# Linear attention in front of two feed-forward stages: scores in 64x64 pieces without the masked quarter, every second tile's decayed k on VectorE, v loaded without padding

## The chip, the cores and the metric

The kernel runs on one core of a Trainium2 chip. The metric is the device time of one execution in microseconds (us), the median of several runs. The engines are called as the profile calls them: PE (TensorE matmul), PEld (its weight loads), DVE (VectorE), ACT (ScalarE), POOL (GpSimd) and SP (SyncE, which here only issues transfers).

## What is computed

Three stages follow one another. The first is a linear attention with decay for 4 sequences of 768 tokens and 8 heads of 48, written in the reference as a loop over tokens:

```python
for t in range(S):
    kt, vt, rt = (k[:, :, t], v[:, :, t], r[:, :, t])
    cur = np.einsum('bhd,bhe->bhde', u[None] * kt, vt)
    y[:, :, t] = np.einsum('bhd,bhde->bhe', rt, state + cur)
    state = w[None, :, :, None] * state + np.einsum('bhd,bhe->bhde', kt, vt)
```

Its output (3072 tokens of 384) goes to a mixture of 8 experts, where each token takes the expert of its largest logit, and from there to a gated feed-forward layer `(silu(x @ w_gate) * (x @ w_val)) @ w_out`.

## The kernel before

**The first stage** works on 24 tiles of 128 tokens, 6 for each sequence. Inside a tile the loop over tokens is a matrix product. r is scaled by powers of the decay (`rdT`), k by inverse powers (`kdT`), both with heads on the partitions, two heads to a pair (rows 0 to 63 and 64 to 127, 48 of each 64 used). The scores of a pair are `kdT` times `rdT`, 128 keys by 128 queries. Only keys before the query count, so half of that square is masked away: `copy_predicated` on DVE puts the scores where the mask is 1 into `dsb`, which holds a diagonal elsewhere (the bonus term with u, from `ck` and its sum `cb`). `psy` is v times `dsb`, plus the state of the earlier tiles times `rdT`. The state itself takes `kdc` (k by token, scaled to the tile's end) times v in `pskv`. `psx` turns the result round and computes the gate logits.

**Who does what in a tile.** POOL makes `ck` in two products, `kdT`, and `kdc` for five tiles in six. DVE makes `rdT`, sums `ck` into `cb`, does two `copy_predicated`, a small sum of logits, and four updates of the state; after each sequence it also does the routing of its tokens in small steps (`advance()`), which stand between the others. ACT makes the eight diagonals of `dsb` from `cb`, and copies `psy` and `psx` out of PSUM. PE does `pss` (scores), `pskv`, `psy` (two lines), `psx`.

**Order.** On PE, DVE, ACT and POOL the instructions of this stage are taken in the order in which the program writes them. The loop runs over `i`; `scaled_r(i + 1)` and `bonus(i + 1)` stand ahead of `scores(i)`, then come `state(i - 1)`, `scaled_k(i + 2)`, `outputs(i - 1)` and `rows_out(i - 2)`. So POOL works two tiles ahead of the scores and DVE one tile ahead. `kdT`, `kdc` and `dsb` have three buffers, `ck` two, the loaded tiles three; `pss` has two PSUM banks that every tile uses again, except tile 1, which has two of its own. SP issues the loads of tile `i + 3` when the instructions that read tile `i` are done.

The second stage starts with a gather of the routed tokens while the last tiles are finished; from there on PE works through the experts and the feed-forward layer.

Of the kernel before, what the change touches and what calls it, by code (L numbers as in the profile page):

```python
# [20 lines left out]
P = 128  # L21
# [17 lines left out]
def moe_kernel(ctx, tc, cst, small, tok, tr, u, w1, w2, m_gate, m_val, m_out, out):  # L39
# [281 lines left out]
    with ExitStack() as actx:  # L321
# [23 lines left out]
            t = bank[:, places[name]]  # L345
            return t if len(dims) == 1 else t.rearrange("p (a b) -> p a b", b=dims[1])

        RK, V, T = 2 * H * D, H * 64, NP * P
        NIO, NV = 3, 4
        io = [carve(RK + 2 * T) for _ in range(NIO)]  # L350
        io_v = [carve(V) for _ in range(NV)]

        def load(i):
            if i < NTILE:
# [3 lines left out]

        def load_v(i):
            if i < NTILE:  # L360
                nc.sync.dma_start(out=io_v[i % NV], in_=tok[i, :, RK:])

        def heads(ap, d=D):
            return ap.rearrange("p (h d) -> p h d", d=d)
# [5 lines left out]
        load(0)  # L370
        nc.sync.dma_start(out=u_tok, in_=u.rearrange("(o h) d -> o h d", o=1).to_broadcast([P, H, D]))
        nc.sync.dma_start(out=cs, in_=cst)
        for i in range(1, NIO):
            load(i)
            load_v(i - 1)
# [13 lines left out]
        def powers():  # L389
            nc.vector.memset(ones, 1.0)  # L390
            nc.vector.memset(pw[:, :, 0:1], 1.0)
            for t in kdc_b:
                nc.gpsimd.memset(t[:, :, D:], 0.0)

            for i in range(WARM):
                wu = ps_m.tile([P, 512], F32, name="wu", tag="m")
# [12 lines left out]
            for q in range(NP):  # L409
                nc.vector.reciprocal(wkT[:, q, :], pw[:, q, 1:])  # L410
                nc.scalar.mul(we[:, q, :], wkT[:, q, :], pw[:, q, P : P + 1])
            pst = ps_m.tile([P, NP, P], F32, name="pst", tag="m")
            for q in range(NP):
                nc.tensor.transpose(pst[:, q, :], we[:, q, :], ident)
            nc.scalar.copy(wk_tok, pst.rearrange("p q (j d) -> p (q j) d", j=2)[:, :, 0:D])
# [23 lines left out]
                )  # L439
            nc.gpsimd.tensor_copy(unit[:, :, D:], wg[:, :, 0:G])  # L440

        S = {}

        def inputs(i):
            t = io[i % NIO]
            r_t, k_t = heads(t[:, 0 : RK // 2]), heads(t[:, RK // 2 : RK])
            rT, kT = pairs(t[:, RK : RK + T]), pairs(t[:, RK + T :])
            rdT = apool.tile([P, NP, P], F32, name="rdT", bufs=3)
            kdT = apool.tile([P, NP, P], F32, name="kdT", bufs=3)
            ck = apool.tile([P, H, D], F32, name="ck")  # L450
            kdc = kdc_b[i % 3]
            S[i] = r_t, k_t, rT, kT, rdT, kdT, ck, kdc

        def scaled_k(i):

# [15 lines left out]
                nc.gpsimd.tensor_tensor(out=ck, in0=ck, in1=r_t, op=ALU.mult)  # L471
            if i:
                nc.gpsimd.tensor_tensor(out=kdT, in0=kT, in1=wkT, op=ALU.mult)  # L473
            if (i + 1) % NCH:
                nc.gpsimd.tensor_tensor(out=kdc[:, :, 0:D], in0=k_t, in1=wk_tok, op=ALU.mult)  # L475

        def scaled_r(i):
            if i >= NTILE:
                return
            r_t, k_t, rT, kT, rdT, kdT, ck, kdc = S[i]  # L480
            if i >= NTILE - 2:
                nc.gpsimd.tensor_tensor(out=rdT, in0=rT, in1=wrT, op=ALU.mult)
            elif i:
                nc.vector.tensor_tensor(out=rdT, in0=rT, in1=wr_ps, op=ALU.mult)
            if i == 1:
                load_v(3)
            load(i + NIO)
            if i == 0:
                load_v(2)

        def bonus(i):
# [5 lines left out]

            dsb = apool.tile([P, H, P], F32, name="dsb", bufs=3)
            for h in [*range(0, H, 2), *range(1, H, 2)]:
                nc.scalar.mul(dsb[:, h, :], ident, cb[:, h : h + 1])  # L500
            S[i] = rdT, kdT, kdc, dsb, heads(io_v[i % NV], 64)

        def scores(i):
            rdT, kdT, kdc, dsb, v_t = S[i]

            if i == 1:
                both = ps_x.tile([P, 2, NP, P], F32, name="pss01", tag="x")
                pss = [both[:, j] for j in range(2)]
            else:
                pss = [ps_s.tile([P, NP, P], F32, name=f"pss{j}", tag="s") for j in range(2)]  # L510
            for q, j in itertools.product(range(NP), range(2)):
                p0 = 64 * j
                nc.tensor.matmul(  # L513
                    pss[j][:, q, :], lhsT=kdT[p0 : p0 + 64, q, :], rhs=rdT[p0 : p0 + 64, q, :], start=True, stop=True
                )
            for j in range(2):
                nc.vector.copy_predicated(
                    dsb.rearrange("p (q j) t -> p q j t", j=2)[:, :, j, :],
                    mask.bitcast(I32).rearrange("p (o t) -> p o t", o=1).to_broadcast([P, NP, P]),
                    pss[j],  # L520
                )
                advance()
                advance()

        def state(i):
# [6 lines left out]
            for q in range(NP):  # L532
                for j in range(2):
                    p0 = 64 * j
                    nc.tensor.matmul(
                        pskv[p0 : p0 + 64, q, :], lhsT=kdc[:, 2 * q + j, :], rhs=v_t[:, 2 * q + j, :],
                        start=True, stop=True,
                    )
            if c == 0:
# [13 lines left out]
        def outputs(i):  # L553
# [4 lines left out]
            for q in range(NP):  # L558
                for j in range(2):
                    p0 = 64 * j  # L560
                    nc.tensor.matmul(  # L561
                        psy[p0 : p0 + 64, q, :], lhsT=v_t[:, 2 * q + j, :], rhs=dsb[:, 2 * q + j, :],
                        start=(q == 0), stop=(c == 0 and q == NP - 1), skip_group_check=True,
                    )
            if c > 0:
# [213 lines left out]
    def sequential(c):  # L779
# [6 lines left out]
        v_d = tok[:, :, 2 * H * D :].rearrange("i t (q j d) -> i j t q d", j=2, d=64)  # L786
# [4 lines left out]
        with tc.For_i(0, B) as b:  # L791
            nc.vector.memset(st, 0.0)
            with tc.For_i(0, NCH) as ch:
# [7 lines left out]
                with tc.For_i(0, P) as t:  # L801
                    kv = sq.tile([P, NP, D], F32, name="sq_kv")
                    for j in range(2):
                        nc.sync.dma_start(
                            out=kv[64 * j : 64 * j + 64],
                            in_=v_d[bass.ds(i, 1), j, bass.ds(t, 1), :, 0:D]
                            .rearrange("o a q d -> (o a) q d").to_broadcast([64, NP, D]),
                        )
                    r_t, k_t = (rk[:, n, :, bass.ds(t, 1)] for n in range(2))
                    nc.vector.tensor_tensor(out=kv, in0=kv, in1=bc(k_t), op=ALU.mult)  # L810
                    cur = sq.tile([P, NP, D], F32, name="sq_cur")
                    nc.vector.tensor_tensor(out=cur, in0=kv, in1=col(up), op=ALU.mult)
                    nc.vector.tensor_tensor(out=cur, in0=cur, in1=st, op=ALU.add)
                    nc.vector.tensor_tensor(out=cur, in0=cur, in1=bc(r_t), op=ALU.mult)
                    psy = ps_m.tile([P, NP], F32, name="sq_psy", tag="m")
                    for q in range(NP):
                        for p0 in (0, 64):
                            nc.tensor.matmul(
                                psy[p0 : p0 + D, q : q + 1], lhsT=cur[p0 : p0 + 64, q, :], rhs=ones[p0 : p0 + 64, :],
                                start=True, stop=True,  # L820
                            )
                    for p0 in (0, 64):
                        pr = slice(p0, p0 + D)
                        nc.vector.tensor_copy(yT[pr, :, bass.ds(t, 1)], psy[pr].rearrange("p (q o) -> p q o", o=1))
                    nc.vector.tensor_tensor(out=st, in0=st, in1=col(wp), op=ALU.mult)
                    nc.vector.tensor_tensor(out=st, in0=st, in1=kv, op=ALU.add)
# [611 lines left out]
EARLY = 3  # L1438
# [54 lines left out]
def _layout(inputs):  # L1493
# [4 lines left out]
    b, h, s, d = r.shape  # L1498
    n = s // P

    def tokens(a, pad=0):
        a = a.transpose(0, 2, 1, 3)
        if pad:
            a = np.concatenate([a, np.zeros(a.shape[:3] + (pad,), a.dtype)], axis=3)
        return a.reshape(b * n, P, -1)

    def pair_rows(a, fill):

# [6 lines left out]
    def transposed(a):  # L1515
# [7 lines left out]
    out = {  # L1523
        "cst": _constants(),
        "small": small,
        "tok": np.concatenate([tokens(r), tokens(k), tokens(v, 64 - d)], axis=2),
        "tr": np.concatenate([transposed(r), transposed(k)], axis=2),
        "u": u,
        "w1": inputs["moe_w1"],
# [27 lines left out]
```

## Time and profile before

| | us |
|---|---|
| median of 3 runs | 800.56 (798.5 to 801.65) |
| the profiled execution | 798.91 |
| its span | 797.2 |
| PE busy | 777.5, 98% of the span |
| DVE busy | 498.1, 62% |
| ACT busy | 346.8, 44% |
| POOL busy | 220.2, 28% |

The profile comes from one execution. Its time stands 1.7 above its span, and its span is what the rows count in. The shares are means over stages that differ: POOL's 28% is nearly all in the first eighth of the span, where it hardly rests. Matmuls are pipelined, so a busy PE need not be PE at its peak, and a matmul's shown length overlaps the next one's.

### The profile page before, as it was taken

The page shows a single profiled execution, that of the slowest core. Times are in us where ns is not written, and L with a number is a line of the kernel's source. Part 1 is how long each engine was busy: PE and PEld are TensorE (multiplying, and loading weights), DVE is VectorE, ACT ScalarE, POOL GpSimd, SP SyncE. Part 2 cuts the span into 40 slices and gives each one's busy share as a digit, 9 for nine tenths or more (in the row PEclk, how much of TensorE's full clock was granted, in tenths as well). Part 3 has the DMA queues.
Part 4 walks back from the last instruction along what each step waited for, and adds up shares of the span by engine and source line. Part 5 has one row for each costly group of instructions (what it writes and reads, how often), then busy time and mean ns, then how long its engine had stood idle before and what let it go on. Part 6 is the DMA issues. An engine that isn't in the chain of part 4 may idle for free.

```text
span 797.2 us, 15589 instructions
## 1 busy us (share of the span) xinstructions
PE 777.5 (98%) x5982; PEld 713.3 (89%) x5983; DVE 498.1 (62%) x1041; ACT 346.8 (44%) x785; POOL 220.2 (28%) x213
## 2 busy tenths in 40 slices
PE   8989998999999999999999999999999999999997
PEld 4878888899999999988888888888888888899997
DVE  7889976889999899787553335334433543344543
ACT  5878873656656656654432223222212221122322
POOL 6999986545233322120002000100200020001000
PEclk9999999999999999999999999999999999999999
DMA  8999974867877784564201000000100000000000
GB/s 321 307 336 339 303 268 142 289 199 220 253 239 238 248 246 144 159 191 140 89 14 40 1 0 14 40 1 1 44 9 1 7 40 1 1 8 40 1 21 24
DMA packets 61860, 99.28 MB, mean 125 GB/s; under 512 B 5461, under 2 KB 48105, under 8 KB 61776
## 3 DMA queue, kind: packets, MB, share of 16 engines
q1 hardware_dynamic: 58320, 88.34, 34.0%
q0 software_dynamic: 3456, 9.85, 3.6%
q8 instruction: 49, 0.80, 0.4%
q14 instruction: 35, 0.29, 0.1%
HBM read 81.64 MB, written 16.53 MB: 123 GB/s over the span
## 4 chain that ended last, share of the span: by engine, by line
issue 54%; PE 29%; POOL 8%; DVE 5%; DMA 1%; ACT 1%; POOLq 0%; SPq 0%; DVEq 0%; ACTq 0%
PE ph L1209 10%; PE py L1209 9%; POOL out_dram L1381 2%; PE pss L513 1%; PE psy L561 1%; POOL kdT L473 1%; POOL kdc L475 1%; PE psy L569 1%; POOL ck L470 1%; PE pya L1209 1%; PE wu L397 1%; POOL ck L471 1%; DMA rw<-m 1%; PE pt L1176 1%; PE pha L1209 1%
## 5 line engine op out<-in xcount | busy, mean ns | idle before, releaser
L1405 PE MATMUL pg<-x,wh 128*128 128x512 f32 (+1 forms) x504 | 146.6, 359 | 0.0
L1410 DVE TENSOR_TENSOR hv<-pg,hv 128x512 f32<-128x512 f32 (+1 forms) x84 | 51.6, 615 | 141.5 <-ACT hv L1409 141.4
L1405 PE MATMUL pv<-x,wh 128*128 128x512 f32 (+1 forms) x504 | 137.7, 358 | 0.0
L1381 POOL DMA_INDIRECT out_dram<-ot,tokd x24 | 24.9, 1038 | 407.1 <-DVE ot L1380 403.4
L1409 ACT ACTIVATE hv<-pg 128x512 f32<-128x512 f32 (+1 forms) x84 | 45.0, 536 | 158.5 <-PE pg L1405 158.1
L968 ACT CAST hh<-hv 128x512 fp32r<-128x512 f32 (+1 forms) x84 | 47.0, 560 | 136.7 <-DVE hv L1411 136.7
L1405 PEld LDWEIGHTS pv<-x,wh 128*128 128x128 f32 x504 | 89.9, 188 | 13.9
L1405 PEld LDWEIGHTS pg<-x,wh 128*128 128x128 f32 x504 | 90.2, 188 | 11.3
L1372 PE MATMUL po<-wh,hl 128*128 128x384 f32 x288 | 97.1, 338 | 0.0
L1372 PE MATMUL po<-wl,hh 128*128 128x384 f32 x288 | 96.8, 336 | 0.0
L1372 PE MATMUL po<-wh,hh 128*128 128x384 f32 x288 | 96.8, 336 | 0.0
L1405 PE MATMUL pg<-x,wl 128*128 128x512 f32 (+1 forms) x252 | 90.3, 358 | 0.0
L1405 PE MATMUL pv<-x,wl 128*128 128x512 f32 (+1 forms) x252 | 90.3, 358 | 0.0
L1209 PE MATMUL ph<-x,w1h 128*128 128x416 f32 (+6 forms) x336 | 87.5, 341 | 0.0
L1209 PE MATMUL py<-h,w2h 128*128 128x416 f32 (+6 forms) x336 | 82.4, 341 | 0.0
L969 DVE TENSOR_TENSOR hl<-hv,hh 128x512 fp32r<-128x512 f32 (+1 forms) x84 | 51.7, 616 | 43.6 <-ACT hh L968 43.3
L1411 DVE TENSOR_TENSOR hv<-pv,hv 128x512 f32<-128x512 f32 (+1 forms) x84 | 51.7, 615 | 38.5 <-PE pv L1405 37.9
L500 ACT ACTIVATE dsb<-cs,cb 128x128 f32<-128x128 f32 x192 | 58.7, 390 | 16.2 <-DVE cb L496 16.0
L1209 PEld LDWEIGHTS ph<-x,w1h 128*128 128x128 f32 x336 | 61.5, 188 | 0.2
L1209 PEld LDWEIGHTS py<-h,w2h 128*128 128x128 f32 x336 | 60.7, 188 | 0.5 <-DVE h L1229 0.3
L1050 POOL TENSOR_TENSOR low<-low,exw 128x384 f32<-128x384 f32 x30 | 32.9, 1098 | 97.7 <-DVE exw L1046 74.2
L1209 PE MATMUL ph<-x,w1l 128*128 128x416 f32 (+6 forms) x168 | 58.4, 348 | 0.7 <-DVE h L1229 0.7
(237 smaller groups left out, 1498.9 us busy)
## 6 DMA issues: line engine op xcount, KB each, us to landing
r<-in_w_dram SPq DMA_DIRECT2D x64, 384.0 KB
yd_all<-in_tr_dram SPq DMA_DIRECT2D x24, 512.0 KB
yd_all<-in_tok_dram SPq DMA_DIRECT2D x24, 384.0 KB
rw<-m SPq DMA_DIRECT2D x36, 192.0 KB
yd_all<-in_tok_dram SPq DMA_DIRECT2D x24, 256.0 KB
m<-ab SPq DMA_DIRECT2D x30, 192.0 KB
x_d<-xt SPq DMA_DIRECT2D x24, 192.0 KB
cva<-in_w_gate_dram SPq DMA_DIRECT2D x10, 384.0 KB
```

Source lines behind the costliest of these rows:

```text
L397: nc.tensor.matmul(wu, lhsT=ones, rhs=ones.rearrange("p (o t) -> p o t", o=1).to_broadcast([P, 4, P]), start=True, stop=True)
L500: nc.scalar.mul(dsb[:, h, :], ident, cb[:, h : h + 1])
L968: first = nc.scalar.copy(hi, src)
L969: second = nc.vector.tensor_tensor(out=lo, in0=src, in1=hi.bitcast(F32), op=ALU.subtract)
L1050: nc.gpsimd.tensor_tensor(out=low, in0=low, in1=ex.bitcast(F32), op=ALU.mult)
L1209: nc.tensor.matmul(dst[:, 0:n], lhsT=a, rhs=b, start=start and t == 0, stop=stop and t == 2)
L1372: mm = nc.tensor.matmul(po[t], lhsT=a[:, t * P : (t + 1) * P], rhs=bb, start=(f == 0 and j == 0), stop=(f == KF2 - 1 and j == 2))
L1381: st = nc.gpsimd.indirect_dma_start(out=out[:, :], out_offset=bass.IndirectOffsetOnAxis(ap=tokd[:, i : i + 1].bitcast(U32), axis=0), in_=o ...
L1405: nc.tensor.matmul(dst, lhsT=a[:, fs], rhs=bb[:, q, :], start=(q == 0 and j == 0), stop=(q == KD - 1 and j == 2))
L1409: nc.scalar.activation(hv, pg, AF.Sigmoid)
L1410: nc.vector.tensor_tensor(out=hv, in0=pg, in1=hv, op=ALU.mult)
L1411: nc.vector.tensor_tensor(out=hv, in0=pv, in1=hv, op=ALU.mult)
```

## The change

Four things change together.

- **Scores.** Each product of 64 rows by 128 keys by 128 queries is cut in two by keys: the first 64 keys with all 128 queries, the last 64 keys with the last 64 queries. The quarter with late keys and early queries is masked anyway and is not computed. So that the two sizes fall alike on both halves of the array's columns, the odd pairs have their tokens in k, v and r by token rolled by 64 on the host, and a second mask and a second diagonal with halves exchanged (`masks`, `idents`) are loaded at the start by three more transfers.
- **kdc.** For tiles 4, 6, ..., 22 the product that makes `kdc` is written in `scaled_r` for DVE, and no longer in `scaled_k` for POOL.
- **v.** It comes with 48 columns for each head instead of 64: 192 KB a tile and not 256. The products still read 64 columns, the last 16 of them the next head's, and what they make of these meets zeros later. Four small fills set the end of each v buffer to zero once.
- **Buffers.** The PSUM banks of the scores are named once at the start, and four of the five warm-up products write them, so that the quarter that no product writes holds numbers.

A loop that runs only for unusual decays was changed to fit and is not reached with these inputs.

```diff
-        RK, V, T = 2 * H * D, H * 64, NP * P
+        RK, V, T = 2 * H * D, H * D, NP * P
...
-        io_v = [carve(V) for _ in range(NV)]
+        io_v = [carve(V + 64 - D) for _ in range(NV)]
+        for t in io_v:
+            nc.gpsimd.memset(t[:, V:], 0.0)
...
+        both = carve(4 * P).rearrange("p (s m t) -> p m s t", s=2, t=P)
+        for to, of in ((slice(0, P),) * 2, (slice(0, 64), slice(64, P)), (slice(64, P), slice(0, 64))):
+            nc.sync.dma_start(
+                out=both[to, :, int(to != of), :], in_=cst[of, 0 : 2 * P].rearrange("p (m t) -> p m t", t=P)
+            )
+        idents, masks = both[:, 0], both[:, 1]
...
+        def by_vector(i):
+            return i > EARLY and i % 2 == 0
...
-            if (i + 1) % NCH:
+            if (i + 1) % NCH and not by_vector(i):
                 nc.gpsimd.tensor_tensor(out=kdc[:, :, 0:D], in0=k_t, in1=wk_tok, op=ALU.mult)
...
                 nc.vector.tensor_tensor(out=rdT, in0=rT, in1=wr_ps, op=ALU.mult)
+            if by_vector(i):
+                nc.vector.tensor_tensor(out=kdc[:, :, 0:D], in0=k_t, in1=wk_tok, op=ALU.mult)
...
-                nc.scalar.mul(dsb[:, h, :], ident, cb[:, h : h + 1])
+                nc.scalar.mul(dsb[:, h, :], idents[:, h // 2 % 2], cb[:, h : h + 1])
...
-            for q, j in itertools.product(range(NP), range(2)):
-                p0 = 64 * j
+            pss = pss_b[i == 1]
+            for q, a, j in itertools.product(range(NP), range(2), range(2)):
+                pr, at = slice(64 * j, 64 * j + 64), 64 * (a ^ q % 2)
                 nc.tensor.matmul(
-                    pss[j][:, q, :], lhsT=kdT[p0 : p0 + 64, q, :], rhs=rdT[p0 : p0 + 64, q, :], start=True, stop=True
+                    pss[j][at : at + 64, q, 64 * a :], lhsT=kdT[pr, q, 64 * a : 64 * a + 64], rhs=rdT[pr, q, 64 * a :],
+                    start=True, stop=True,
                 )
```

How the change moves instructions shows in the written order of three engines. First POOL, before, from `kdT` of tile 5 to `kdc` of tile 7 (EARLY is 3, so tile 6 is one of those that change):

```order
L473 TENSOR_TENSOR kdT<-yd_all 128x512
L470 TENSOR_TENSOR ck<-yd_all 128x384
L471 TENSOR_TENSOR ck<-ck,yd_all 128x384
L473 TENSOR_TENSOR kdT<-yd_all 128x512
L475 TENSOR_TENSOR kdc_146<-yd_all 128x8x48
L470 TENSOR_TENSOR ck<-yd_all 128x384
L471 TENSOR_TENSOR ck<-ck,yd_all 128x384
L473 TENSOR_TENSOR kdT<-yd_all 128x512
L475 TENSOR_TENSOR kdc_147<-yd_all 128x8x48
```

The same place on POOL in the changed kernel:

```order
L489 TENSOR_TENSOR kdT<-yd_all 128x512
L486 TENSOR_TENSOR ck<-yd_all 128x384
L487 TENSOR_TENSOR ck<-ck,yd_all 128x384
L489 TENSOR_TENSOR kdT<-yd_all 128x512
L486 TENSOR_TENSOR ck<-yd_all 128x384
L487 TENSOR_TENSOR ck<-ck,yd_all 128x384
L489 TENSOR_TENSOR kdT<-yd_all 128x512
L491 TENSOR_TENSOR kdc_154<-yd_all 128x8x48
```

`kdc` of tile 6 is gone from POOL, that of tile 7 stays, and `ck` of tile 7 moves up behind `kdT` of tile 6. DVE, before, from `rdT` of tile 6 to `rdT` of tile 7:

```order
L484 TENSOR_TENSOR rdT<-yd_all,wr_ps 128x512
L496 TENSOR_REDUCE cb<-ck 128x8
L517 COPY_PREDICATED dsb<-cs,pss_605 128x4x128
L517 COPY_PREDICATED dsb<-cs,pss_606 128x4x128
L133 TENSOR_REDUCE yd_all<-lh 128x16
L545 SCALAR_TENSOR_TENSOR st_145<-st_144,yd_all,pskv 128x64 x4
L484 TENSOR_TENSOR rdT<-yd_all,wr_ps 128x512
```

And in the changed kernel (the state's four updates make two rows there):

```order
L500 TENSOR_TENSOR rdT<-yd_all,wr_ps 128x512
L502 TENSOR_TENSOR kdc_153<-yd_all 128x8x48
L514 TENSOR_REDUCE cb<-ck 128x8
L532 COPY_PREDICATED dsb<-yd_all,pss_163 128x4x128
L532 COPY_PREDICATED dsb<-yd_all,pss_164 128x4x128
L133 TENSOR_REDUCE yd_all<-lh 128x16
L560 SCALAR_TENSOR_TENSOR st_152<-st_151,yd_all,pskv 128x64 x4
L500 TENSOR_TENSOR rdT<-yd_all,wr_ps 128x512
```

`kdc` of tile 6 now stands between `rdT` and `cb` of tile 6, ahead of the two copies of tile 5. PE, before, from `psx` to `pskv` around one tile's scores:

```order
L126 MATMUL psx<-unit,yT 64x64 x16
L513 MATMUL pss_516<-rdT,kdT 128x128
L513 MATMUL pss_517<-rdT,kdT 128x128
L513 MATMUL pss_516<-rdT,kdT 128x128
L513 MATMUL pss_517<-rdT,kdT 128x128
L513 MATMUL pss_516<-rdT,kdT 128x128
L513 MATMUL pss_517<-rdT,kdT 128x128
L513 MATMUL pss_516<-rdT,kdT 128x128
L513 MATMUL pss_517<-rdT,kdT 128x128
L535 MATMUL pskv<-yd_all,kdc_146 64x64 x8
```

In the changed kernel the first of four such pieces (there is one for each pair, all alike in the listing):

```order
L126 MATMUL psx<-unit,yT 64x64 x16
L527 MATMUL pss_163<-rdT,kdT 64x128
L527 MATMUL pss_164<-rdT,kdT 64x128
L527 MATMUL pss_163<-rdT,kdT 64x64
L527 MATMUL pss_164<-rdT,kdT 64x64
```

Eight products of 128 by 128 became sixteen, half of them 64 by 128 and half 64 by 64; the places of all other products are the same. The trace shows each fp32 product as two passes.

## Rows read from the trace of the kernel before

**Rows 1.** The page, busy us of each engine, its share of the span, instructions:

```profile
PE 777.5 (98%) x5982; PEld 713.3 (89%) x5983; DVE 498.1 (62%) x1041; ACT 346.8 (44%) x785; POOL 220.2 (28%) x213
```

**Rows 2.** Windows: stretch, length, busy of each engine, PE clock, DMA share, GB/s:

```profile
core 0: us, PE busy (x) PEld busy (x) DVE busy (x) ACT busy (x) POOL busy (x), PEclk, DMA share, GB/s
24.23:113.50 89.27, 84.74 (x1955) 76.17 (x1951) 78.64 (x226) 71.28 (x223) 86.75 (x84) 1.00 0.94 324
113.50:160.00 46.50, 42.33 (x412) 39.88 (x405) 31.95 (x102) 25.36 (x64) 27.78 (x24) 1.00 0.63 200
160.00:797.20 637.20, 630.87 (x3446) 585.49 (x3444) 369.28 (x673) 235.17 (x456) 88.98 (x78) 1.00 0.27 83
```

**Rows 3.** Waits from 24.23 to 113.5: who for whom, us, times, longest:

```profile
DVE cb L496 <- POOL ck L471: 5.4, 5, 1.6
DVE dsb L517 <- PE pss L513: 3.2, 5, 1.1
...
PE bank L220 <- DVE sel L216: 2.7, 3, 1.2
...
DVE rk L188 <- PE bank L178: 0.9, 1, 0.9
...
POOL ck L470 <- DMA yd_all<-in_tok_dram: 0.3, 1, 0.3
```

**Rows 4.** Timeline of POOL: start, us, engine, line, operation, tiles, idle before:

```profile
37.17 1.27 POOL L473 TENSOR_TENSOR kdT<-yd_all 128x512 f32<-128x512 f32 x1
38.40 1.01 POOL L475 TENSOR_TENSOR kdc<-yd_all 128x384 f32<-128x384 f32 x1
39.37 0.99 POOL L470 TENSOR_TENSOR ck<-yd_all 128x384 f32<-128x384 f32 x1
```

**Rows 5.** Timeline of DVE, tiles 7 and 8 of the first stage:

```profile
35.83 0.68 DVE L484 TENSOR_TENSOR rdT<-yd_all,wr_ps 128x512 f32<-128x512 f32 x1
37.24 0.55 DVE L496 TENSOR_REDUCE cb<-ck 128x8 f32<-128x384 f32 x1 [0.73 <-POOL ck L471]
...
39.24 0.69 DVE L484 TENSOR_TENSOR rdT<-yd_all,wr_ps 128x512 f32<-128x512 f32 x1
41.48 0.55 DVE L496 TENSOR_REDUCE cb<-ck 128x8 f32<-128x384 f32 x1 [1.56 <-POOL ck L471]
```

**Rows 6.** Timeline of DVE, two products with both inputs in SBUF:

```profile
176.43 1.52 DVE L1052 TENSOR_TENSOR low<-ab,low 128x384 f32<-128x384 f32 x1
...
184.00 0.56 DVE L1052 TENSOR_TENSOR low<-ab,low 128x384 f32<-128x384 f32 x1 [0.41 <-POOL low L1050]
184.48 0.95 DVE L1079 TENSOR_TENSOR w2l<-r,w2h 128x768 fp32r<-128x768 f32 x1
```

**Rows 7.** Timeline of POOL around the first of these:

```profile
175.71 1.81 POOL L746 TENSOR_TENSOR dsel<-dsel,cs 128x576 bf16<-128x576 f32 x1 [0.70 <-DVE dsel L743]
177.49 4.12 POOL L751 TENSOR_TENSOR dsel<-dsel,scale 128x576 bf16<-128x576 f32 x3
```

**Rows 8.** Timeline of PE, one tile; a form is rows*columns of the array:

```profile
61.21 0.98 PE L569 MATMUL psy<-rdT,st 64*64 64x128 f32 x14
61.93 0.27 PE L126 MATMUL psx<-unit,yT 64*64 64x64 f32 x2
62.02 0.28 PE L569 MATMUL psy<-rdT,st 64*64 64x128 f32 x2
62.03 0.73 PE L126 MATMUL psx<-unit,yT 64*64 64x64 f32 x30
62.69 1.16 PE L513 MATMUL pss<-rdT,kdT 64*128 64x128 f32 x16
63.78 0.44 PE L561 MATMUL psy<-dsb,yd_all 128*64 128x128 f32 x4
```

**Rows 9.** Timeline of DVE in the first tiles:

```profile
10.88 0.57 DVE L467 TENSOR_TENSOR bank<-yd_all 128x384 f32<-128x384 f32 x1 [0.75 <-DMA yd_all<-in_tok_dram]
...
20.08 0.55 DVE L496 TENSOR_REDUCE cb<-ck 128x8 f32<-128x384 f32 x1 [1.36 <-POOL ck L471]
```

More of the change, by code (lines that the diff above doesn't have):

```diff
@@ L360, in load_v @@
             if i < NTILE:
-                nc.sync.dma_start(out=io_v[i % NV], in_=tok[i, :, RK:])
+                nc.sync.dma_start(out=io_v[i % NV][:, 0:V], in_=tok[i, :, RK:])
         def heads(ap, d=D):
@@ L393, in powers @@
                 nc.gpsimd.memset(t[:, :, D:], 0.0)
+            pss_b.append([ps_s.tile([P, NP, P], F32, name=f"pss{j}", tag="s") for j in range(2)])
+            both = ps_x.tile([P, 2, NP, P], F32, name="pss01", tag="x")
+            pss_b.append([both[:, j] for j in range(2)])
             for i in range(WARM):
-                wu = ps_m.tile([P, 512], F32, name="wu", tag="m")
+                wu = pss_b[i // 2][i % 2].rearrange("p q t -> p (q t)") if i < 4 else ps_m.tile([P, 512], F32, name="wu", tag="m")
                 nc.tensor.matmul(
@@ L410, in powers @@
                 nc.vector.reciprocal(wkT[:, q, :], pw[:, q, 1:])
-                nc.scalar.mul(we[:, q, :], wkT[:, q, :], pw[:, q, P : P + 1])
+                for a in range(1 + q % 2):
+                    to, of = (slice(0, P),) * 2 if q % 2 == 0 else (slice(64 * a, 64 * a + 64), slice(64 - 64 * a, P - 64 * a))
+                    nc.scalar.mul(we[:, q, to], wkT[:, q, of], pw[:, q, P : P + 1])
             pst = ps_m.tile([P, NP, P], F32, name="pst", tag="m")
@@ L440, in units @@
             nc.gpsimd.tensor_copy(unit[:, :, D:], wg[:, :, 0:G])
-        S = {}
+        S, pss_b = {}, []
         def inputs(i):
@@ L499, in bonus @@
             for h in [*range(0, H, 2), *range(1, H, 2)]:
-                nc.scalar.mul(dsb[:, h, :], ident, cb[:, h : h + 1])
-            S[i] = rdT, kdT, kdc, dsb, heads(io_v[i % NV], 64)
+                nc.scalar.mul(dsb[:, h, :], idents[:, h // 2 % 2], cb[:, h : h + 1])
+            S[i] = rdT, kdT, kdc, dsb, [io_v[i % NV][:, h * D : h * D + 64] for h in range(H)]
         def scores(i):
             rdT, kdT, kdc, dsb, v_t = S[i]
[L506 to L510, printed above, removed]
-            for q, j in itertools.product(range(NP), range(2)):
-                p0 = 64 * j
+            pss = pss_b[i == 1]
+            for q, a, j in itertools.product(range(NP), range(2), range(2)):
+                pr, at = slice(64 * j, 64 * j + 64), 64 * (a ^ q % 2)
                 nc.tensor.matmul(
-                    pss[j][:, q, :], lhsT=kdT[p0 : p0 + 64, q, :], rhs=rdT[p0 : p0 + 64, q, :], start=True, stop=True
+                    pss[j][at : at + 64, q, 64 * a :], lhsT=kdT[pr, q, 64 * a : 64 * a + 64], rhs=rdT[pr, q, 64 * a :],
+                    start=True, stop=True,
                 )
@@ L517, in scores @@
                 nc.vector.copy_predicated(
-                    dsb.rearrange("p (q j) t -> p q j t", j=2)[:, :, j, :],
-                    mask.bitcast(I32).rearrange("p (o t) -> p o t", o=1).to_broadcast([P, NP, P]),
-                    pss[j],
+                    dsb.rearrange("p (o s j) t -> p o s j t", s=2, j=2)[:, :, :, j, :],
+                    masks.bitcast(I32).rearrange("p (o s) t -> p o s t", o=1).to_broadcast([P, NP // 2, 2, P]),
+                    pss[j].rearrange("p (o s) t -> p o s t", s=2),
                 )
@@ L535, in state @@
                     nc.tensor.matmul(
-                        pskv[p0 : p0 + 64, q, :], lhsT=kdc[:, 2 * q + j, :], rhs=v_t[:, 2 * q + j, :],
+                        pskv[p0 : p0 + 64, q, :], lhsT=kdc[:, 2 * q + j, :], rhs=v_t[2 * q + j],
                         start=True, stop=True,
@@ L561, in outputs @@
                     nc.tensor.matmul(
-                        psy[p0 : p0 + 64, q, :], lhsT=v_t[:, 2 * q + j, :], rhs=dsb[:, 2 * q + j, :],
+                        psy[p0 : p0 + 64, q, :], lhsT=v_t[2 * q + j], rhs=dsb[:, 2 * q + j, :],
                         start=(q == 0), stop=(c == 0 and q == NP - 1), skip_group_check=True,
@@ L785, in sequential @@
         col = lambda ap: bc(ap.rearrange("p (q o) -> p q o", o=1))
-        v_d = tok[:, :, 2 * H * D :].rearrange("i t (q j d) -> i j t q d", j=2, d=64)
+        v_d = tok[:, :, 2 * H * D :].rearrange("i t (q j d) -> i j t q d", j=2, d=D)
         ones = sq.tile([P, 1], F32, name="sq_one")
@@ L800, in sequential @@
                 nc.vector.memset(yT, 0.0)
[L801 to L816, printed above, removed]
-                        for p0 in (0, 64):
[L818 to L826, printed above, removed]
@@ new lines, in sequential @@
+                for a in range(2):
+                    with tc.For_i(0, 64) as s:
+                        t = s + 64 * a
+                        kv = sq.tile([P, NP, D], F32, name="sq_kv")
+                        for j, o in itertools.product(range(2), range(2)):
+                            nc.sync.dma_start(
+                                out=kv[64 * j : 64 * j + 64, o::2, :],
+                                in_=v_d[bass.ds(i, 1), j, bass.ds(s + 64 * (a ^ o), 1), o::2, 0:D]
+                                .rearrange("o a q d -> (o a) q d").to_broadcast([64, NP // 2, D]),
+                            )
+                        r_t, k_t = (rk[:, n, :, bass.ds(t, 1)] for n in range(2))
+                        nc.vector.tensor_tensor(out=kv, in0=kv, in1=bc(k_t), op=ALU.mult)
+                        cur = sq.tile([P, NP, D], F32, name="sq_cur")
+                        nc.vector.tensor_tensor(out=cur, in0=kv, in1=col(up), op=ALU.mult)
+                        nc.vector.tensor_tensor(out=cur, in0=cur, in1=st, op=ALU.add)
+                        nc.vector.tensor_tensor(out=cur, in0=cur, in1=bc(r_t), op=ALU.mult)
+                        psy = ps_m.tile([P, NP], F32, name="sq_psy", tag="m")
+                        for q in range(NP):
+                            for p0 in (0, 64):
+                                nc.tensor.matmul(
+                                    psy[p0 : p0 + D, q : q + 1], lhsT=cur[p0 : p0 + 64, q, :], rhs=ones[p0 : p0 + 64, :],
+                                    start=True, stop=True,
+                                )
+                        for p0 in (0, 64):
+                            pr = slice(p0, p0 + D)
+                            nc.vector.tensor_copy(yT[pr, :, bass.ds(t, 1)], psy[pr].rearrange("p (q o) -> p q o", o=1))
+                        nc.vector.tensor_tensor(out=st, in0=st, in1=col(wp), op=ALU.mult)
+                        nc.vector.tensor_tensor(out=st, in0=st, in1=kv, op=ALU.add)
@@ L1499, in _layout, with tokens @@
     n = s // P
[L1501 to L1505, printed above, removed]
+    def tokens(a):
+        a = a.transpose(0, 2, 1, 3).reshape(b * n, P, h // 4, 2, 2, d)
+        return np.stack([a[:, :, :, 0], np.roll(a[:, :, :, 1], 64, axis=1)], axis=3).reshape(b * n, P, -1)
     def pair_rows(a, fill):
@@ L1525, in _layout @@
         "small": small,
-        "tok": np.concatenate([tokens(r), tokens(k), tokens(v, 64 - d)], axis=2),
+        "tok": np.concatenate([tokens(r), tokens(k), tokens(v)], axis=2),
         "tr": np.concatenate([transposed(r), transposed(k)], axis=2),
```

## The prediction

> **What bounds the kernel now.** First the page's busy times: PE works 98% of the span and all others far less [rows 1]. That is a mean over stages, so the windows come next. From 160 us on PE is busy 630.9 of 637.2 us and nothing in the change touches that part; it moves as a block to wherever the first stage ends. From 24.2 to 113.5 us the first stage runs evenly, and there the shares are others: POOL 86.8 of 89.3 us, PE 84.7, DVE 78.6, ACT 71.3, the DMA engines 94% [rows 2]. Four engines and the DMA lie within a fifth of each other, so no single relief can give much, and whatever is put on a relieved engine's neighbour counts. The question is which engine waits for which. The list of waits answers it: in this stretch DVE waits 5.4 us for POOL's `ck`, 3.2 us for the scores on PE and 0.9 us for PE's routing products; PE waits 2.7 us for DVE's routing; POOL waits for nothing but 0.3 us of a load [rows 3]. So POOL paces the even stretches, and DVE paces the tiles in which a sequence is routed. DVE's idle time is 89.3 - 78.6 = 10.6 us: 5.4 for POOL, 4.1 for PE, and 1.1 in gaps too small for the list.
>
> **The change part by part.**
>
> *POOL.* Ten `kdc` go (tiles 4 to 22). One starts 0.97 us ahead of the next instruction (38.40 to 39.37) [rows 4], so POOL loses 9.7 of its 86.8 us and no longer paces: 77.1 us, 80 or so with the delays below. DVE's 5.4 us of waiting for `ck` go with it.
>
> *DVE.* Ten products of 128x384 with both inputs in SBUF come. The trace of before has none at this place; the nearest is L1052, the same size and sources, which took 0.56 us and held the next instruction for 0.48 (184.00 to 184.48) while POOL was idle [rows 6]. That is 4.8 us for ten, the bound from below. But one L1052 took 1.52 us [rows 6], and POOL was then in an operation that ran to 175.71 + 1.81 = 177.52; DVE ended 0.43 us after it, at 177.95 [rows 7]. DVE had waited for POOL's operation to end. `rdT`, which has one input in PSUM, takes 0.68 to 0.69 us beside a POOL that hardly rests [rows 5], so it is the second SBUF input that costs. The Trainium skill says so too (SBUF — State Buffer, Who interferes with whom): a DVE instruction with two SBUF inputs and a GpSimd instruction that reads SBUF shut each other out, and the first holds to its end. The trace agrees by the 1.52 against 0.56.
>
> How long does the new `kdc` wait? POOL's operations here last 0.99 to 1.27 us [rows 4] back to back, so the wait lies between 0 (it comes as one ends) and 1.27 (as one starts). Without a reason for either end I take half of a mean one, 0.5 us, so 0.98 us for each and 9.8 us for ten. The other way round, POOL is held up to 0.48 us each time, 4.8 us at most and 3 by my choice; it has those 9.7 us to pay them from.
>
> So DVE's work becomes 78.6 + 9.8 = 88.4 us in a stretch of 89.3. Its waits for POOL go, those for PE mostly go as well (DVE is later, the scores come sooner), the small gaps of 1.1 stay: 89.5 us, 0.2 more than now. DVE has taken POOL's place as the engine that paces. Queued behind `kdc` on DVE are `cb` of the same tile, for which ACT's eight diagonals wait, and the two copies of the tile before, which free the PSUM banks for PE's next scores.
>
> *PE.* One tile's scores hold PE from 62.69 to 63.78, 1.09 us for 16 passes [rows 8]. Now there are 32 passes, half with 128 columns and half with 64, in the 64*64 form, in which four can run at once. Three quarters of 1.09 is 0.82, the bound from below. From above: L569 has 16 passes of 128 columns in 0.72 us (61.21 to 61.93), 45 ns each, and `psx` 32 of 64 columns in 0.76 (to 62.69), 24 ns each [rows 8]; 16 of each are 1.10 us, no gain. I take 0.9: nearer to the lower bound, since `psx` keeps all four parts at work and the two sizes alternate between the halves. That is 0.2 us for each of 24 tiles. PE has 4.5 us of idle time in the stretch anyway [rows 2], so this buys no time there; it shortens DVE's waits, and only the last tile's scores, behind which PE alone remains, give their 0.2 to the end.
>
> *v.* 64 KB less for each of 24 tiles, 5% of a tile's 1344 KB (loads of 512, 384 and 256, a store of 192). Loads made POOL wait 0.3 us in all [rows 3], so it is worth at most that; I count 0.1. The work that hides it is everything else.
>
> *At the start.* Three transfers with 256 KB more stand on SP's queue ahead of the loads of tile 1. At the 324 GB/s of the stretch [rows 2] that is 0.8 us for what follows. DVE waited 0.75 us for tile 1's `tok`, which then came at 10.88, and will wait some 0.8 more; but at 20.08 it waits 1.36 us for POOL anyway [rows 9], and POOL's own chain starts from other inputs. Nothing for the end, 0.8 if that cover fails. The four fills run while POOL waits for the first load. The copies through a mask and the diagonals keep their sizes: nothing.
>
> *Sum.* +0.2 (DVE) - 0.2 (last scores) - 0.1 (loads) = -0.1 us, against the profiled execution's own 798.91. That execution lay 1.65 us under the median of the three runs, so I carry the difference over to 800.56: about 800.4. Where a `kdc` falls into a wait for `ck` that still stands, it costs less than 0.98; I put 0.2 for that: 800.2 us.
>
> **The rivals.**
>
> *Faster: DVE's new product fits into waits that it has already.* It stands directly ahead of `cb`, and that is the instruction that waits for POOL: 0.73 us at 37.24, 1.56 at 41.48 [rows 5]. If POOL's operations end just as DVE asks, each `kdc` costs its bare 0.48: 78.6 + 4.8 + 1.1 = 84.5 us, 4.8 under now, with 0.3 from the end and the loads about 795.5. For it speaks that these waits are there; against it, that they are waits for the very engine that must then be idle, and that the routing stretches have none. It decides below a wait of 0.1 us a product.
>
> *Slower: the two engines shut each other out for whole operations.* If DVE asks, each time, just after POOL has begun, it waits a mean operation, 1.07 us: 78.6 + 10 x 1.55 + 1.1 = 95.2 us, 5.9 more, about 806.2. POOL, held in turn, is not early with the next `ck`. For it speaks that both engines are nearly full, so that they meet at every product, and that the order is fixed, so that the same meeting can repeat ten times. Against it: POOL will rest some 9 us, and a product that falls there waits for nothing. It passes +0.5% from a wait of 0.9 us. This is the case that the skill's page above would lead to where POOL always issues first.
>
> *Slower: the small scores don't overlap.* If 32 passes go at the 68 ns of the old ones (1.09 / 16), a tile takes 2.18 us; 24 x 1.09 = 26 us more on a PE with 4.5 to spare, about 820. Against it stand `psx`'s 24 ns in the same form [rows 8].
>
> **How the numbers follow.** About 0.5% (4 us) is what a measurement of this kernel can tell from no change: the three runs spread over 3.2 us. The balance above is the likeliest, 0.63; DVE's waits as cover 0.20; whole operations 0.14; scores that don't overlap 0.03. From the same cases: faster by over 0.5% 0.20, within 0.5% 0.63, slower by over 0.5% 0.17. The likeliest case has its own range from the wait: 0.2 us gives 86.5, 2.8 us under now, and 0.8 us gives 92.5, 3.2 over: with the 0.3 from the end and the loads 797.5 to 803.5. The range given reaches into both other cases, 796.2 to 804.3.
>
> **What would show it.** In the profile of after: POOL's busy time in the first stage down by 7 to 10 us, with idle time in it that ends with DVE or PE; L502 on DVE ten times, with a mean of 0.8 to 1.2 us and single ones between 0.55 and 1.8; DVE's wait for `ck` under 2 us and DVE near 98% busy; the scores of a tile from their first pass to the next line's in 0.82 to 1.0 us; and the time behind the first stage as before. A mean of L502 below 0.65 would mean the faster rival, above 1.4 the slower one. The sum is wrong if POOL still paces (its waits empty, DVE waiting for `ck`), if a load becomes the last wait, or if the time behind 113.5 changes.

## The result and the profile after

The changed kernel takes 808.09 us (median of 6 runs, 806.9 to 810.56) against 799.88 for the kernel before on the same chip (6 runs, 798.35 to 801.65): a ratio of 1.0102, 95% interval 1.0085 to 1.0119, or 8.2 us slower. The prediction was 800.2, range 796.2 to 804.3. The profiled execution took 806.9 us, its span 805.0.

The windows of the changed kernel over the first stretch of [rows 2], and over one in which the clock fell:

```profile
core 0: us, PE busy (x) PEld busy (x) DVE busy (x) ACT busy (x) POOL busy (x), PEclk, DMA share, GB/s
24.23:113.50 89.27, 77.87 (x2169) 69.56 (x2161) 82.30 (x228) 69.86 (x222) 74.72 (x70) 0.96 0.87 297
...
82.00:88.00 6.00, 6.00 (x98) 5.41 (x100) 3.96 (x12) 3.10 (x10) 5.75 (x6) 0.50 0.77 271
```

POOL is relieved, from 86.75 to 74.72 us, and DVE has more, 82.30. But no engine fills the stretch any longer: PE, which worked 84.74 us of it, now works 77.87. The stage still has some way to go at 113.5: the last `psx` starts at 123.88 here. Since 805.0 - 123.88 = 681.1 us follow it, and in the kernel before 797.2 - 116.97 = 680.2 (the timelines of PE, both shown below), 6.9 us of the 7.8 between the two spans are lost in the first stage.

What engines wait for, in the changed kernel from 24 to 130 us (who for whom, us in all, times, longest):

```profile
POOL ck L486 <- DMA yd_all<-in_tok_dram: 6.2, 8, 1.9
...
PE psx L126 <- issue: 5.4, 3, 2.6
...
DVE dsb L532 <- PE pss L527: 4.3, 3, 3.2
POOL kdc L491 <- PE pskv L550: 3.9, 2, 3.1
PE pss L527 <- issue: 3.0, 6, 1.7
...
PE psy L584 <- issue: 1.3, 2, 0.7
...
PE psy L576 <- issue: 1.0, 1, 1.0
```

DVE's wait for `ck`, 5.4 us in [rows 3], is gone, as forecast. Two things are new. POOL waits 6.2 us for `tok`, the load that brings the input of `ck`. And PE stands still for "issue", which is no semaphore that the profile shows: 5.4 + 3.0 + 1.3 + 1.0 = 10.7 us; in the kernel before the same list has 0.8 us, in `psx`. The timeline of PE shows how such a stop looks; the first row is the scores of tile 3, long before it, the second the line that follows them:

```profile
24.82 0.90 PE L527 MATMUL pss<-rdT,kdT 64*64 64x128 f32 x32
25.66 0.69 PE L550 MATMUL pskv<-yd_all,kdc 128*64 128x64 f32 x16
...
78.78 0.50 PE L126 MATMUL psx<-unit,yT 64*64 64x64 f32 x11
81.88 0.90 PE L126 MATMUL psx<-unit,yT 64*64 64x64 f32 x19 [2.60 <-issue]
...
83.03 1.56 PE L527 MATMUL pss<-rdT,kdT 64*64 64x128 f32 x32
84.52 1.12 PE L550 MATMUL pskv<-yd_all,kdc 128*64 128x64 f32 x16
...
122.32 0.73 PE L126 MATMUL psx<-unit,yT 64*64 64x64 f32 x30
123.88 0.69 PE L126 MATMUL psx<-unit,yT 64*64 64x64 f32 x32
```

PE stops in the middle of one line, between products that read the same `yT` and `unit`. Afterwards its clock is granted at 0.50 for 82 to 88 us (1.2 GHz in place of 2.4), and the scores' line takes 84.52 - 83.03 = 1.49 us in place of the 0.84 of 24.82 to 25.66. The last row is the last tile's `psx`. In the kernel before, the scores of tile 3 and the last `psx` are these two:

```profile
23.66 1.16 PE L513 MATMUL pss<-rdT,kdT 64*128 64x128 f32 x16
...
116.97 0.69 PE L126 MATMUL psx<-unit,yT 64*64 64x64 f32 x32
```

Where the stops fall is told by counting. These windows of the changed kernel run from the end of one stop to the end of a later one:

```profile
39.50:45.80 6.30, 4.67 (x126) 4.12 (x127) 5.17 (x10) 5.18 (x17) 5.27 (x6) 1.00 0.92 301
45.80:51.16 5.36, 4.21 (x127) 3.83 (x126) 3.83 (x15) 3.57 (x11) 4.91 (x6) 1.00 0.95 315
51.16:61.20 10.04, 8.38 (x252) 7.62 (x253) 9.79 (x30) 7.69 (x24) 7.53 (x8) 1.00 0.84 294
...
66.05:81.85 15.80, 13.20 (x379) 11.91 (x379) 15.39 (x40) 13.60 (x44) 12.80 (x13) 0.99 0.91 311
```

PE has 127 products and 126 weight loads in one of them, twice that in the third, three times in the last: each of these stops stands a whole number of steps of 253 recorded instructions after the one before. And the queue that the profile calls "instruction" moved one packet of 16 KB for about each such step. From 24 to 110 us, first the kernel before, then the changed one (packets, MB, share):

```profile
q8 instruction: 14, 0.23, 1.0%
```

```profile
q8 instruction: 16, 0.26, 1.3%
```

The changed kernel has 2169 + 2161 recorded instructions on PE in the stretch and still isn't through; the kernel before had 1955 + 1951 [rows 2]. The scores' 32 passes with 32 weight loads make each tile's share of PE's program a sixth longer (112 passes in place of 96). The reading that follows is that PE comes to the end of a piece of its program before the next one is there; e4 and e8 below put it to the test. The Trainium skill (Runtime: NRT & Kernel Launch, Instruction fetch mechanics) says that an engine's program is fetched in blocks of 256 instructions by a DMA queue of its own while the block before runs, at a cost "mostly hidden". The trace agrees with the block (steps of 253 recorded instructions, packets of 16 KB); by this reading 10.7 us are not hidden here.

### The profile page after: what moved, and what is told of

Read it like the earlier page. It is cut to its first block, busy times and chain, and to the rows that moved or that the text cites. A ratio compares the mean times of both kernels' runs of the same rounds, so it can differ in the third digit from the quotient of the medians.

```text
span 805.0 us, 16373 instructions
## 1 busy us (share of the span) xinstructions
PE 772.8 (96%) x6366; PEld 710.3 (88%) x6367; DVE 503.5 (63%) x1051; ACT 347.4 (43%) x787; POOL 213.5 (27%) x207
## 4 chain that ended last, share of the span: by engine, by line
issue 55%; PE 20%; DVE 10%; POOL 6%; DMA 5%; ACT 2%; SPq 1%; POOLq 0%; DVEq 0%; ACTq 0%
PE ph L1226 6%; PE py L1226 5%; POOL out_dram L1398 2%; DMA m<-ab 2%; PE psy L576 2%; PE psy L584 1%; PE pss L527 1%; PE pya L1226 1%; PE pskv L550 1%; DMA rw<-m 1%; DVE w2l L1096 1%; PE psx L126 1%; DVE ab L1070 1%; PE pha L1226 1%; DMA yd_all<-in_tok_dram 1%
## 5 line engine op out<-in xcount | busy, mean ns | idle before, releaser
L518 ACT ACTIVATE dsb<-yd_all,cb 128x128 f32<-128x128 f32 x192 | 58.8, 392 | 15.8 <-DVE cb L514 15.5
```

What stands on the lines that cost most here:

```text
L518: nc.scalar.mul(dsb[:, h, :], idents[:, h // 2 % 2], cb[:, h : h + 1])
```

## The experiments

Theory 1 (code): PE waits for pieces of its own program, because 32 passes make it longer. Theory 2 (slot): the load of tile i+3 now waits for DVE's `kdc` of tile i, where it waited for a POOL that ran ahead, and comes late for `ck`. The forecast's own theory was DVE and POOL shutting each other out. The runs form three groups, each on a chip of its own, so ratios are compared, and each is to the kernel before on the same chip; a difference in us is that ratio times the median of the kernel before.

**First group: e1 to e4.** The kernel before had a median of 805.24 us on this chip.

e1, `kdc` on DVE alone:

```diff
-            if (i + 1) % NCH:
+            if (i + 1) % NCH and not by_vector(i):
...
+            if by_vector(i):
+                nc.vector.tensor_tensor(out=kdc[:, :, 0:D], in0=k_t, in1=wk_tok, op=ALU.mult)
```

> The kernel before with one part of the change: kdc of the even tiles from 4 on DVE. TensorE's program is that of before. Theory 1 (code: TensorE now waits for pieces of its own program, because the scores' 32 passes make it longer): no new stops of PE, the time within 1.5 us of before, since L502 took a mean of 0.84 us in the changed kernel. Theory 2 (slot: the load of tile i+3 waits for DVE's kdc of tile i where it waited for POOL's, and lands too late for POOL's ck): POOL waits for tok some 5 to 7 us in the first stage, and the time is 3 to 7 us over before.

Ratio 1.0012 (0.9988 to 1.0037), 1.0 us. POOL waits 2.0 us for `tok`, two times, and PE 2.0 us for "issue". Theory 2 has little left of its 3 to 7.

e2, the changed kernel with `by_vector` always false:

> The changed kernel with kdc back on POOL for all tiles; the small scores, the packed v and the loads at the start stay. Theory 1 (code): PE's stops at every 253rd recorded instruction or so stay, and the time stays 4 to 9 us over before. Theory 2 (slot): POOL's wait for tok falls under 1 us and the time comes back to within 1.5 us of before, but for some 1 us of the loads at the start.

Ratio 1.0065 (1.004 to 1.009), 5.2 us, and the stops are there. PE's waits for "issue" in e2 from 24 to 130 us, 10.1 us in all:

```profile
PE psx L126 <- issue: 4.9, 4, 2.0
PE pss L527 <- issue: 2.2, 3, 1.0
PE psy L584 <- issue: 2.0, 2, 1.6
PE pskv L550 <- issue: 1.0, 3, 0.4
```

POOL's wait for `tok` is down to 1.3 us, but the time doesn't come back, as theory 2 wanted.

e3, the changed kernel with fewer instructions elsewhere on PE:

```diff
-        for q, (j, k) in itertools.product(range(NP), ((0, 0), (1, 1), (0, 1), (1, 0))):
-            pr, ts = slice(64 * j, 64 * j + 64), slice(64 * k, 64 * k + 64)
-            nc.tensor.matmul(psx[ts, j, q, :], lhsT=yT[pr, q, ts], rhs=unit[pr, q, :], start=True, stop=True)
+        for q, j in itertools.product(range(NP), range(2)):
+            pr = slice(64 * j, 64 * j + 64)
+            nc.tensor.matmul(psx[:, j, q, :], lhsT=yT[pr, q, :], rhs=unit[pr, q, :], start=True, stop=True)
```

> The changed kernel with psx in 16 passes of 128 tokens by 64 columns in place of 32 of 64 by 64, the same products. A tile then has 96 passes on PE as before the change, and not 112. Theory 1 (code): PE's stops of over 1 us between instructions of one line go, the granted clock stays 1.00, and of the 8 us some 5 to 7 come back: 800 to 803. Theory 2 (slot) and the forecast's theory (DVE and POOL shutting each other out): nothing that PE's instruction count touches, so 807 to 809, or more if the 16 passes are slower than the 32.

Ratio 1.0048 (1.0022 to 1.0074), 3.9 us. The stops are gone; PE's whole wait for "issue" in e3 from 24 to 130 us is this line:

```profile
PE pskv L550 <- issue: 0.7, 2, 0.4
```

But less came back than theory 1 said: the 3.9 us that stay can't be told from e2's 5.2. POOL waits 5.9 us for `tok`, nearly as in the changed kernel. What the 16 passes cost of their own was open; e6 is for that.

e4, the kernel before with more instructions on PE:

```diff
-                            psy[pr, q, :], lhsT=st_b[i % 2][pr, q, :], rhs=rdT[pr, q, :], start=False, stop=(q == NP - 1),
...
+                        for a in range(2):
+                            ts = slice(64 * a, 64 * a + 64)
...
+                                psy[pr, q, ts], lhsT=st_b[i % 2][pr, q, :], rhs=rdT[pr, q, ts], start=False,
...
```

> The kernel before with the 16 passes of 128 columns of psy from the state cut in two: 32 of 64 columns, the same products and columns. A tile then has 112 passes as in the changed kernel; DVE, POOL and the loads are as before. Theory 1 (code): stops of over 1 us appear on PE at every 250th recorded instruction or so, and the time is 3 to 7 us over before. Theory 2 and the forecast's: the time stays within 1.5 us of before, for PE has 4.5 us of idle time in the stage.

Ratio 1.0113 (1.0074 to 1.0151), 9.1 us, more than expected. PE's waits for "issue" in e4 from 24 to 130 us:

```profile
PE pskv L535 <- issue: 2.9, 4, 1.3
PE pss L513 <- issue: 1.7, 3, 0.9
PE psy L561 <- issue: 1.1, 1, 1.1
PE psy L571 <- issue: 0.4, 1, 0.4
```

6.1 us of stops, with nothing changed but PE's program. It isn't all of the 9.1: cut in two, these passes hold PE from 62.11 to 63.04, 0.93 us, where the uncut ones took 0.72 [rows 8]. Over 24 tiles that is 5.0 us more of PE's own work, so e4 shows where the stops come from and not what they cost.

**Second group: e5 to e8.** Before: 797.5 us. e5 is the kernel before with the change's three loads of `cst` behind that of `cs`, e6 the edit of e3 in the kernel before. e7 and e8 are the kernel before and the changed kernel with `if i < 9:` in `load` and `load_v`: from tile 9 on they compute with old data, so the output is another, and what follows the first stage may be too: their totals (1183.3 and 1185.6 us) say nothing, and only the first stage of one execution each is read.

> The kernel before with the three loads of masks and diagonals at the start and nothing else of the change; what they bring isn't read. Theory 1 says that the start is a part of its own: tile 1's tok lands about 1.0 us later, DVE's first rdT starts 1.2 us later as in the changed kernel, and the whole is 1.0 to 2.0 us slower. The forecast said that the wait at 20.08 covers it: 0.3 us at most.

Ratio 0.9991 (0.9979 to 1.0002). DVE's `bank` for tile 1 starts at 11.89 there, as in the changed kernel (11.88) and a microsecond later than in [rows 9], and yet nothing is lost: the forecast's cover holds, and theory 1's 1.0 to 2.0 us for the start was wrong. PE waits 2.4 us for "issue" in this run, also without a loss.

> The kernel before with psx in 16 passes of 128 tokens by 64 columns. It takes apart why the run with 16 passes in the changed kernel gave back less than forecast though the stops went. If the 16 passes cost PE more than the 32 did (the profile of that run has PE busy 87.5 of 90 us, L126 up from 17.5 to 23.3 us), this is 2 to 6 us over before, with no stops on PE. If the rest lay elsewhere, the time stays within 1.5 us of before.

Ratio 1.0096 (1.0065 to 1.0127), 7.7 us, with no stop for "issue" in the stage. The groups of L126 on PE from 24 to 114 us, in e6 and then in the kernel before (form, shape, count, busy us and mean ns, idle before):

```profile
L126 PE MATMUL psx<-unit,yT 64*128 64x64 f32 x320 | 22.2, 278 | 0.0
```

```profile
L126 PE MATMUL psx<-unit,yT 64*64 64x64 f32 x672 | 18.0, 225 | 0.8 <-issue 0.8
```

Half as many passes take longer in all, and PE is busy 88.9 of 90 us. So e3 traded the stops for a fuller PE, and its 3.9 us are no measure of what the stops cost.

> The kernel before without the loads of tiles 9 to 23: from there on every tile computes with what its buffers hold, so the output is another and the routing may be. It is the control for the next run. Theory 1: from 55 us on the first stage keeps its pace (POOL paces it, not a load), so the gather starts within 1.5 us of where it did, 109.3. If loads did hold the kernel before, it comes sooner.

> The changed kernel without the loads of tiles 9 to 23, as in the control. Theory 1, with the rider that the pieces of the program are late because they queue among the loads: the stops of over 1 us on PE go once the loads have ended (from some 45 us on), the granted clock stays 1.00, and the first stage ends 3 to 5 us sooner than in the changed kernel, within some 2 us of the control. If the stops stay with the loads gone, the pieces are late for a reason of their own. Theory 2 (slot): POOL's wait for tok goes too, but PE's stops stay.

The last `psx` of the stage in e7, and then in e8, there with the last stop for "issue" that PE has ahead of it (timelines of PE):

```profile
115.75 0.69 PE L126 MATMUL psx<-unit,yT 64*64 64x64 f32 x32
```

```profile
42.04 0.76 PE L576 MATMUL psy<-dsb,yd_all 128*64 128x128 f32 x9 [0.99 <-issue]
...
119.52 0.69 PE L126 MATMUL psx<-unit,yT 64*64 64x64 f32 x32
```

The control ends its stage 1.2 us sooner than the kernel before, so loads hardly held that. e8 ends it 4.4 us sooner than the changed kernel (2.6 sooner than e12, the second execution of it, at 122.14), and the row at 42.04 is its last stop on PE, though its program is as long as ever: without the loads' traffic (DMA share 0.30 from 45 us on) the pieces come in time. So it takes both, a longer program and loads among which its pieces queue. The rider of 2 us fails: e8 is 3.8 us behind the control, of which 1.7 were there at the `psx` of tile 8 (57.68 against 56.02). The other 2.1 came without any stop, and the profile shows what came instead. PE waits for `sel`, a result of DVE's routing, in e8 and then in e7, from 24 to 125 us:

```profile
PE bank L220 <- DVE sel L216: 5.9, 3, 2.8
```

```profile
PE bank L220 <- DVE sel L216: 2.1, 3, 1.2
```

All three waits of e8 lie behind the `psx` of tile 8. So with the stops gone it is DVE, which has `kdc` in e8, that PE waits for in the tiles with routing. The expected clock of 1.00 failed too: after the wait of 1.59 us that ended at 85.28, it was granted at 0.50 from 88 to 90 us.

**Third group: e9 to e12.** Before: 797.14 us. e9 is the packed `v` alone; e10 the changed kernel with the scores, masks and diagonals of before, and so PE's old program (the PSUM banks of the scores and the warm-up are those of before too); e11 the kernel before with packed `v` and `kdc` on DVE where `i % 4 == 0`; e12 the changed kernel again.

> The kernel before with the packed v alone: 1536 bytes a row in place of 2048, and four fills at the start. Forecast and theory 1: 0.1 us, at most 0.3 gained, so within 1 us of before; the loads are shorter, so a piece of the program may come sooner, which can only help. If shorter rows made the loads worse, POOL's wait for tok would rise over 2 us and the time with it.

Ratio 1.0002 (0.9992 to 1.0012).

> The changed kernel with the scores of before: kdc on DVE, packed v and the three loads at the start stay, the 16 passes of 128 columns come back, and with them PE's program of before. Theory 1 (code): the time is within 2.5 us of before and the stops of over 1 us at most two. If the parts other than the scores together cost the 8 us, as theory 2 needs (kdc on DVE behind later loads), it is 5 us or more over before.

Ratio 1.0018 (1.0004 to 1.0031), 1.4 us.

> A version that might beat both: the kernel before with packed v and kdc on DVE for tiles 4, 8, 12, 16 and 20 alone. POOL gives 5 x 0.97 = 4.9 of its 86.8 us, DVE takes 5 x 0.84 = 4.2 on its 78.6, so that neither fills the 89.3 us, and PE's program stays. PE with 84.7 us is then the next bound: 1 to 4 us under before if the three are evenly loaded, 0 if they wait for each other as they do now.

Ratio 1.0007 (0.9994 to 1.002): no gain. DVE still waits 1.9 us for `ck` and 3.1 us for the scores there, so it may be that the three engines wait for each other as before; that was not taken apart. No version beat the kernel before.

> The changed kernel itself, beside the one with the scores of before on the same chip. All theories: 7 to 9 us over before, with the stops on PE where they were by count of instructions (1200, 1453, 1706, 2211, 3222, 4486), but of other lengths.

Ratio 1.0078 (1.006 to 1.0097), 6.2 us, somewhat under the expected 7 to 9. PE's waits for "issue" from 24 to 130 us, in e10 and in e12:

```profile
PE pskv L547 <- issue: 0.9, 2, 0.7
PE psx L126 <- issue: 0.4, 1, 0.4
```

```profile
PE psx L126 <- issue: 3.6, 3, 1.9
PE psy L584 <- issue: 2.8, 2, 1.7
PE pss L527 <- issue: 1.1, 3, 0.7
PE psy L576 <- issue: 0.7, 2, 0.4
```

On one chip, then, the small scores are 6.2 - 1.4 = 4.8 us of the change's loss, and with them the stops go from 1.3 to 8.2 us. The other runs with all loads and PE's program of before have 0.8 to 2.4. The stops fall at the same passes in both executions of the changed kernel, on two chips; here is one in the first and then in e12, each with 26 passes of that `psx` left:

```profile
45.84 0.62 PE L126 MATMUL psx<-unit,yT 64*64 64x64 f32 x26 [1.62 <-issue]
```

```profile
45.72 0.62 PE L126 MATMUL psx<-unit,yT 64*64 64x64 f32 x26 [1.89 <-issue]
```

POOL waits 5.2 us for `tok` in e10 too, and the whole of e10 costs 1.4; in e12 it waits 1.6, and the loss is there. So that wait is not what the change loses. Theory 2 falls.

The two profiled executions don't show the 4.8 as they stand: e10's is its slowest (801.23 us), e12's among its fastest (801.73). e10's scores of tile 3 start only at 26.81, 1.77 us behind those of e12, and what came ahead of them is not the scores' doing. The table below therefore counts from there.

## Why the prediction was wrong

**The step that failed is PE's.** It priced the 32 passes by the array alone, 0.82 to 1.10 us a tile, and let PE's 4.5 us of idle time absorb whatever came. The array's part was right, at its lower bound (0.84 us); what had no term is the program that PE has to fetch for them, 9.9 us more of stops in the first run, and a granted clock that falls after a long one. The small scores, which were to cost nothing, cost 4.8 us (e12 less e10), the larger part of the loss. The sum's -0.2 for the last scores is worth nothing beside it. The rows for it were there in part: [rows 2] counts PE's instructions, and the kernel before has 0.8 us of waits for "issue" within `psx`, which can be read as pieces that came only just in time.

PE's own account shows what became of the 4.5 us of idle time and of the array's gain. It runs from the start of tile 3's scores to the start of the last `psx`, 93.31 us in the kernel before, in one execution each, all against the kernel before: the stops are the waits for "issue"; the clock is what the windows with a clock under 1 lack; the scores are 21 tiles of 1.09 - 0.84 us; other waits are those on PE's list for another engine or line in the first stage.

| | from, to | longer | stops | clock | scores | other waits | sum |
|---|---|---|---|---|---|---|---|
| changed, first run | 24.82, 123.88 | 5.8 | +9.9 | +3.4 | -5.3 | -2.0 | 6.0 |
| e12, changed again | 25.04, 122.14 | 3.8 | +7.4 | +1.7 | -5.3 | -0.4 | 3.4 |
| e2, `kdc` on POOL | 26.51, 120.98 | 1.2 | +9.3 | 0 | -5.3 | -3.0 | 1.0 |
| e10, old scores | 26.81, 121.04 | 0.9 | +0.5 | +0.1 | 0 | +0.1 | 0.7 |
| e1, `kdc` on DVE alone | 24.53, 120.53 | 2.7 | +1.2 | 0 | 0 | +0.2 | 1.4 |

In four of five the terms give the length to 0.4 us; in e1 1.3 us stay unexplained. The rows are of single executions, that of e2 being the fastest of its ten (805.63 us, with a median of 808.37). So the small scores did give PE 5.3 us and the stops took more than that. Where the stops stood in for other waits and the clock stayed up (e2), little was lost in this stretch; the first run, with a long time at the lower clock, lost most.

**DVE's step held within its range.** L502 in the changed kernel, with its least, middle and longest ns:

```profile
L502 DVE TENSOR_TENSOR kdc<-yd_all x10: 539/706/1539, 26.0 to 104.7; 128x384 f32<-128x384 f32 x10
```

The mean is 0.84 us (0.98 forecast; 1.13 in e1), from a bare 0.54 to 1.54, which is about a whole operation of POOL's in waiting. DVE does not fill the stretch: 82.30 of 89.27 us, where 98% was forecast. PE's stops can be only a part of that, for with few of them it is 83.89 in e10 and 85.41 in e1. All but the scores costs 1.4 us in e10, inside the 2.8 under to 3.2 over of the likeliest case, though more than the sum's +0.2 for DVE. Neither rival came: the mean is far from the 1.4 of whole operations, and the kernel did not get faster by `kdc` fitting into old waits.

**POOL's step held in size, not in what ends its rests.** It lost 12 us in the stretch (77 to 80 forecast, 74.72 measured, partly since fewer tiles lie in it). The largest part of its rests, 6.2 of 14.6 us, ends with a load, which the prediction named as a sign that the sum is wrong. The sum was, but not by this: e10 has 5.2 us of it and costs little.

**The start and v held.** e5 finds nothing at the end for the three loads, e9 nothing for the packed `v`; both terms were 0 and 0.1. The time behind the first stage is 0.9 us longer, about as before.

**What stays open.** The first run lost 8.2 us and e12 6.2, with intervals that overlap. In both the granted clock fell to 0.50 after one of the longest stops: from 82 to 88 us in the first, after 2.60 us, and from 48 to 50 us in e12, after 1.89. No experiment takes the slower clock and the stops apart, but the record allows an estimate beyond the two traces. The mean granted clock was 0.991 over the six runs of e12, 0.995 over the twelve of e10 and 0.996 over the 29 of the kernel before; span times what is missing to 1 gives 7.0, 3.7 and 3.0 us. So up to 3.3 of the 4.8 us may be time at the lower clock. A fall needs no stop for "issue": in e1 one came at 164 us, after a wait of 2.29 us for DVE. It was not tried to have the pieces of the program fetched earlier.

## What to carry to other kernels

Cutting products into smaller ones is not free where the array has room: count PE's instructions before and after, and look whether the list of waits has "issue" on PE in the middle of a line. If it has, further instructions can cost more than the array gains by them while loads are in flight. And a long stop can cost again through the granted clock behind it. Relieving the pacing engine by its neighbour gave nothing here, where the neighbour was nearly as full (e1, e11).

## What the runs showed that was not expected

PE's longer stops stand whole steps of 253 recorded instructions apart, as if its program came in pieces, and such a stop can last 2.60 us while the DMA engines are about 90% busy. Taking the loads away ended the stops (e8); adding instructions alone brought them (e4); and they came back at the same passes on another chip (e12). After the stop of 2.60 us PE's clock was granted at 0.50 from 82 to 88 us, though PE was busy for all of these 6 us. And for `psx`, passes in the 64*64 form cost less than half as many in the 64*128 form: 18.0 against 22.2 us of PE for 672 and 320 passes.
